# An fp32 attention and two-layer MLP kernel: the sign of half the weight conversions is made by GpSimd instead of VectorE

## The chip, the cores and the metric

The kernel runs on one core of a Trainium2 chip. The metric is the device time of one execution in microseconds, as the median of several runs. TensorE (PE in the profile) multiplies matrices, VectorE (DVE) and ScalarE (ACT) work elementwise, GpSimd (POOL) works elementwise on SBUF only, and SyncE (SP) issues all the DMAs. Each engine takes its own instructions strictly in the order of the program and waits at the first one whose inputs are not there.

## The reference

Three stages follow each other. `q`, `k` and `v` have the shape (4, 8, 576, 64); 4 x 576 = 2304 tokens, each 8 x 64 = 512 wide.

```
scores = where(mask, q @ k.T / 8, -1e9)       # heads 0-3: the last 32 keys; heads 4-7: every 32nd key
x  = softmax(scores) @ v                      # 2304 x 512
x  = relu(x @ w_in)**2 @ w_out                # 512 -> 2048 -> 512
h  = x @ w_in2                                # 512 -> 2048
g  = (a0 + a1 h + a2 h^2 + a3 h^3) / (1 + |b0||h| + |b1| h^2 + 1e-6)
out = g @ w_out2                              # 2048 -> 512
```

The weights arrive as 8-byte floats, and the kernel turns them into 4-byte floats on the chip.

## The kernel before

**Precision.** A matrix product of 4-byte accuracy is built from three fast ones. Each operand is split into a high part (rounded to the fast format) and a low part (the rest), and a tile of the product is the sum of high x high, high x low and low x high. So every weight tile needs `wh` and `wl`, every activation tile `xh`, `xl` or `gh`, `gl`.

**Blocks.** The tokens are worked in five blocks (512, 384, 512, 512 and 384 tokens in the first layer). In a block there are 16 units, one for each 128 of the 2048 hidden features. Unit `f` computes `h` (12 matmuls, line 423), squares it on ScalarE, splits it into `gh` and `gl`, and two units later adds its part to four output accumulators `acc` (12 matmuls, line 468). Names in the listings below carry block and unit: `h_0_2` is block 0, unit 2; `wh_2` and `wl_2` are the weights of unit 2. The second layer is the same with lines 423 and 658.

**Conversion of weights.** The first layer's weights are converted once, while block 0 runs: 32 conversions, (unit, part), part 0 being the columns for `h` and part 1 those for `acc`. Their order is the list `wq`: (0,0), (1,0), (2,0), (0,1), (3,0), (1,1), (4,0), ... alternating from there on, until the last ones are all of part 1. `feed_w` issues two in each unit. One conversion is a chain over three engines (`to_f32`, lines 177 to 192, then `split_w`, line 198):

- ScalarE, line 188: `w` = the absolute value of the upper 4-byte word, scaled, which moves the exponent into place;
- VectorE, line 189: `bits` = `w` shifted left by 3, without the sign bit (`bits` lies in PSUM);
- VectorE, line 190: the sign bit of the upper word is put in;
- VectorE, line 191: the top 3 bits of the lower word are put in; the result is written over the raw tile or over `w`;
- GpSimd, lines 200 and 201: `wh` and then `wl`.

**Attention.** It is cut into 13 pieces (`ORDER`). For a piece, TensorE computes scores into two PSUM banks, VectorE subtracts the maximum (line 339), ScalarE takes the exponential (line 340), VectorE sums (lines 341 to 343), GpSimd scales (line 344), TensorE transposes (line 352), ScalarE copies back (line 354), and TensorE multiplies by `v` (line 361). The tiles are called `eas`/`es` (strided heads) or `eal`/`el` (local heads). Three pieces come before block 0 starts (to about 30 us), three more (numbers 3 to 5) run inside it, the others later. Pieces with a number under `MASK_PE` (line 236) get their mask by a matmul of an identity with the mask into the bank (line 295), onto which the scores are added; for the others VectorE adds the mask to the scores (line 329).

**The order of work.** The code is written unit by unit; a scheduler then puts the instructions of each engine in an order by its own estimate of when they can start, apart from those that the kernel pins with `keep_in_program_order` (the attention matmuls of the first three pieces, the conversions' ScalarE step in block 0, the second layer's elementwise work). Changed instructions can so change places with others on their engine. `fill` (line 486) puts matmuls of ones into TensorE's stream in front of some steps of the first pieces.

**The end.** In the second layer `split2` (line 640) makes `gh` on ScalarE and `gl` on GpSimd (line 645) for each unit. The last unit is (4, 14), a double unit of 256 tokens; the last 24 matmuls of the program use it.

Of the kernel before, what the change touches and what calls it, by code (L numbers as in the profile page):

```python
# [9 lines left out]
F32 = mybir.dt.float32  # L10
# [4 lines left out]
ALU = mybir.AluOpType  # L15
# [13 lines left out]
NB2 = len(WIDTHS2)  # L29
FSTEP = [512 // w for w in WIDTHS2]  # L30
STARTS2 = tuple(sum(WIDTHS2[:j]) for j in range(NB2 + 1))
NF = DFF // P
# [89 lines left out]
def moe_kernel(ctx, tc, qs, vs, ql, vl, w1, w2, a, b, masks, eye, out):  # L122
    nc = tc.nc
# [49 lines left out]
    def in_order(which, ins):  # L173
        if which and block0[0]:
            tc.keep_in_program_order(ins)

    def to_f32(layer, f, part, raw, place=None):

        lo, hi = raw[:, :, 0], raw[:, :, 1]
        w = stage.tile([P, DM], I32, tag="w32", bufs=3, name=f"w32_{layer}_{f}_{part}")
        bits, to = w, w
        if layer == 0 and place:
            to = hi
        if layer == 0:
            bits = psum_w.tile([P, DM], I32, tag="bits", name=f"bits{f}_{part}")
        in_order(layer == 0, nc.scalar.activation(w.bitcast(F32), hi.bitcast(F32), AF.Abs, scale=2.0**-112))
        nc.vector.tensor_scalar(bits, w, 3, 0x7FFFFFFF, ALU.logical_shift_left, ALU.bitwise_and)
        nc.vector.scalar_tensor_tensor(bits, hi, -0x80000000, bits, ALU.bitwise_and, ALU.bitwise_or)  # L190
        nc.vector.scalar_tensor_tensor(to, lo, 29, bits, ALU.logical_shift_right, ALU.bitwise_or)
        return to.bitcast(F32)

    def w_place(layer, f):
        wt[layer, f] = tuple(wpool.tile([P, 2 * DM], F32R, tag=f"w{c}{f}", name=f"w{c}{layer}_{f}") for c in "hl")
        return wt[layer, f]

    def split_w(wh, wl, wf):

        nc.gpsimd.tensor_scalar(wh, wf, 1.0, 0.0, ALU.mult, ALU.add)  # L200
        nc.gpsimd.tensor_tensor(wl, wf, wh.bitcast(F32), ALU.subtract)
# [31 lines left out]
    ORDER = [("s", 0, 2), ("s", 0, 3), ("l", 0), ("l", 1), ("s", 1, 2), ("s", 1, 3), ("l", 2),  # L233
             ("s", 2, 2), ("s", 2, 3), ("l", 3), ("s", 3, 2), ("s", 3, 3), ("l", 4)]
    pieces = [Piece(n, *x) for n, x in enumerate(ORDER)]
    HEAD, MASK_PE = 3, 6
    for p in pieces[:HEAD]:
        p.pinned = True
    pieces[0].homes = ("l8", "l9")
# [262 lines left out]
    def load_co():  # L502
# [9 lines left out]
    homes = [  # L512
        ("h8", 0), ("h9", 0), ("h15", 0), ("h14", 0), ("h13", 0), ("h12", 0), ("l15", 0), ("l14", 0), ("l13", 0), ("l12", 0), ("l9", 1), ("l8", 1),
        ("h11", 1), ("l11", 1), ("h10", 1), ("l10", 1),
    ]
    homes += [(x, 1) for x in ("h12", "h13", "h14", "h15", "l15", "l14", "l13", None, None, None, "h15", "l15")] + [(None, 1)] * 4
    raws = []

    def load_raw(done):

        while len(raws) < min(len(wq), done + AHEAD):
            k = len(raws)
            place, free = homes[k]
            if phase < free or place and any(homes[i][0] == place for i in range(done, k)):
                break
            raws.append(load_w(0, *wq[k], place=place and "w" + place))

    fed = [0]
    AHEAD = 8

    def feed_w(n):
        for _ in range(n):
            load_raw(fed[0])
            if fed[0] < len(wq):
                f, part = wq[fed[0]]
                c = slice(part * DM, (part + 1) * DM)
                wh, wl = wt[0, f] if part else w_place(0, f)
                split_w(wh[:, c], wl[:, c], to_f32(0, f, part, raws[fed[0]], homes[fed[0]][0]))
                fed[0] += 1

    phase, under_way[0] = 0, 2_200_000
# [14 lines left out]
    load_qk(pieces[3])  # L556
    at_out(P0)
    feed_w(1)
    at_transpose(P1, 0)
    at_transpose(P1, 1)  # L560
    at_values(P1)
    at_out(P1)
    load_v(pieces[3])
    feed_w(1)
    at_transpose(P2, 0)
    at_transpose(P2, 1)
    at_values(P2)
    at_out(P2)
    phase, under_way[0] = 1, 0
    load_raw(fed[0])  # L570
    feed_w(1)
    steps = [(j, f) for j in range(NB) for f in range(NF)]
    prev = []
# [3 lines left out]
    def spill_w(f, part):  # L577

        wf = to_f32(1, f, part, load_w(1, f, part))
        parts = [stage.tile([P, DM], F32R, tag="w32", bufs=3, name=f"sp{c}{f}_{part}") for c in "hl"]  # L580
        split_w(*parts, wf)
        for z, t in enumerate(parts):
            nc.sync.dma_start(w2_dram[z, f][:, part * DM : (part + 1) * DM], t.bitcast(F32))
# [5 lines left out]
    keep = tc.keep_in_program_order  # L589
# [50 lines left out]
    def split2(n):  # L640
        if len(open2) > n:
            j, f, rq = open2.pop(0)
            gh, gl = (l2.tile([P, 512], F32R, tag=f"g{c}2", name=f"g{c}1_{j}_{f}", bufs=4) for c in "hl")
            keep(nc.scalar.copy(gh, rq))  # L644
            keep(nc.gpsimd.tensor_tensor(gl, rq, gh.bitcast(F32), ALU.subtract))  # L645
            gt[1, j, f] = gh, gl

    def o_unit2(j, f):
# [26 lines left out]
    def unit2(j, f):  # L675
        ps = psum.tile([P, 512], F32, tag="ps", name=f"h1_{j}_{f}")
        for d in range(FSTEP[j]):
            h_unit(1, j, f + d, ps)
        act2(j, f, ps)
        split2(2)  # L680
        if j + 1 < NB2 and f in X_AT[j > 0]:
            load_x1(j + 1, X_AT[j > 0].index(f))
        prev2.append((j, f))
# [71 lines left out]
    for j, f in [(j, f) for j in range(NB2) for f in range(0, NF, FSTEP[j])][EARLY:]:  # L755
        unit2(j, f)
        while len(prev2) > LAG2:
            o_unit2(*prev2.pop(0))
    multiply2()
    split2(1)  # L760
    split2(0)
    for u in prev2:
        o_unit2(*u)
# [19 lines left out]
```

## Time and profile before

| | us |
|---|---|
| median of 3 runs | 856.35 |
| lowest, highest | 855.86, 857.38 |
| the profiled execution | 857.55 |
| its span, first to last instruction | 855.8 |
| block 0 of the first layer | about 30 to 137 |
| second layer alone | about 475 to 852 |

A sum that starts from the trace starts from 857.55 us. The page lists busy time by engine; queries give the stretch, the waits and the single instructions. TensorE is called busy while any matmul is in flight, and the matmuls overlap in its pipeline: a 512-wide matmul is shown as 0.39 us, but in a dense stretch the next one starts 0.23 us later. So starts are compared, not lengths. VectorE's instructions overlap a little too.

### The profile page before, as it was taken

The numbers are of one execution on the slowest core, as the hardware profiler recorded it, in microseconds if no ns is written. First come the engines' busy times: TensorE is split into PE (matmuls) and PEld (weight loads), VectorE is DVE, ScalarE is ACT, GpSimd is POOL, SyncE is SP. The second block draws the span as 40 slices with busy tenths as digits, with TensorE's granted clock in tenths as the row PEclk, the third lists the DMA queues.
The fourth block names the chain that finished last, engine by engine and source line by source line (L and its number), as shares of the span: only waits on it lengthen the run. The fifth ranks groups of instructions, "written<-read, shape, count | busy, mean of one in ns | idle before, by whom it ended". The sixth has DMA issues, their size and how long they took to land.

```text
span 855.8 us, 14872 instructions
## 1 busy us (share of the span) xinstructions
PE 846.5 (99%) x5762; PEld 720.0 (84%) x5762; DVE 600.3 (70%) x688; ACT 453.6 (53%) x821; POOL 523.2 (61%) x468
## 2 busy tenths in 40 slices
PE   7999999999999999999999999999999999999998
PEld 4788889999888888889999888888888888888896
DVE  5899856556556555552127688888888888888885
ACT  3556534333333343333346566676667666766673
POOL 1687754455444465664334687778777777777664
PEclk9999999999999999999999999999999999999999
DMA  9972535555343374565774300010001000100010
GB/s 338 358 246 78 171 122 200 165 178 188 109 148 106 101 242 156 193 197 194 263 256 148 137 24 25 12 62 13 14 12 62 7 7 6 57 1 0 1 51 25
DMA packets 38246, 99.99 MB, mean 117 GB/s; under 512 B 4384, under 2 KB 8224, under 8 KB 38176
## 3 DMA queue, kind: packets, MB, share of 16 engines
q1 hardware_dynamic: 38176, 99.05, 34.3%
q8 instruction: 45, 0.74, 0.3%
q14 instruction: 25, 0.20, 0.1%
HBM read 72.82 MB, written 26.21 MB: 116 GB/s over the span
## 4 chain that ended last, share of the span: by engine, by line
PE 98%; DVE 1%; DMA 0%; ACT 0%; issue 0%; POOL 0%; SPq 0%; ACTq 0%; POOLq 0%
PE h L423 46%; PE acc L468 23%; PE acc L658 23%; PE ps_vl L361 1%; PE ps_sl L300 1%; PE ps_vs L361 1%; PE ps_ss L300 1%; PE ps_tl L352 1%; PE ps_ts L352 1%; DMA cst<-in_masks 0%; DVE sm L330 0%; PE ps_tl L490 0%; DVE sm L341 0%; PE ps_ss L295 0%; PE ps_sl L295 0%; DVE eal L339 0%
## 5 line engine op out<-in xcount | busy, mean ns | idle before, releaser
L423 PE MATMUL h<-xh,wh 128*128 128x512 f32 (+2 forms) x640 | 237.0, 371 | 0.0
L423 PE MATMUL h<-xh,wl 128*128 128x512 f32 (+2 forms) x640 | 235.6, 368 | 0.0
L423 PE MATMUL h<-xl,wh 128*128 128x512 f32 (+2 forms) x640 | 235.6, 368 | 0.0
L629 DVE RECIPROCAL h<-w 128x512 f32<-128x512 f32 x67 | 224.6, 3353 | 0.0
L624 POOL TENSOR_TENSOR p<-p,hs 128x512 f32<-128x512 f32 x67 | 86.9, 1297 | 97.6 <-ACT p L622 97.5
L423 PEld LDWEIGHTS h<-xh,wh 128*128 128x128 f32 x640 | 120.4, 188 | 18.3 <-issue 0.5
L423 PEld LDWEIGHTS h<-xh,wl 128*128 128x128 f32 x640 | 120.3, 188 | 17.7
L423 PEld LDWEIGHTS h<-xl,wh 128*128 128x128 f32 x640 | 120.4, 188 | 17.5
L468 PE MATMUL acc<-gh,wh 128*128 128x512 f32 (+1 forms) x320 | 118.2, 369 | 0.0
L468 PE MATMUL acc<-gh,wl 128*128 128x512 f32 (+1 forms) x320 | 117.7, 368 | 0.0
L468 PE MATMUL acc<-gl,wh 128*128 128x512 f32 (+1 forms) x320 | 117.6, 367 | 0.0
L658 PE MATMUL acc<-wh,gh 128*128 128x512 f32 x288 | 112.2, 389 | 0.0
L658 PE MATMUL acc<-wh,gl 128*128 128x512 f32 x288 | 112.2, 389 | 0.0
L658 PE MATMUL acc<-wl,gh 128*128 128x512 f32 x288 | 112.1, 389 | 0.0
L619 ACT ACTIVATE sq<-h 128x512 f32<-128x512 f32 x72 | 43.0, 597 | 128.3 <-PE h L423 122.0
L446 POOL TENSOR_TENSOR gl<-r,gh 128x512 fp32r<-128x512 f32 (+1 forms) x59 | 69.5, 1178 | 63.6 <-ACT gh L445 58.4
L627 DVE SCALAR_TENSOR_TENSOR p<-p,co,h 128x512 f32<-128x512 f32 x72 | 53.6, 745 | 69.2 <-POOL p L624 69.2
L438 ACT ACTIVATE r<-h 128x512 f32<-128x512 f32 (+1 forms) x75 | 41.8, 558 | 112.7 <-PE h L423 112.7
L442 DVE TENSOR_TENSOR r<-r 128x512 f32<-128x512 f32 (+1 forms) x59 | 43.6, 739 | 76.3 <-ACT r L438 76.2
L645 POOL TENSOR_TENSOR gl<-rq,gh 128x512 fp32r<-128x512 f32 x72 | 93.4, 1298 | 3.2 <-ACT gh L644 3.2
L626 POOL TENSOR_TENSOR w<-w,sq 128x512 f32<-128x512 f32 x66 | 85.5, 1296 | 0.0
L445 ACT CAST gh<-r 128x512 fp32r<-128x512 f32 (+1 forms) x75 | 43.7, 583 | 57.4 <-DVE r L442 56.9
(115 smaller groups left out, 1324.2 us busy)
## 6 DMA issues: line engine op xcount, KB each, us to landing
wraw<-in_w SPq DMA_DIRECT2D x64, 512.0 KB, 4.3
w_scratch<-sph SPq DMA_DIRECT2D x32, 256.0 KB, 3.9
w_scratch<-spl SPq DMA_DIRECT2D x32, 256.0 KB, 3.2
wh<-w_scratch SPq DMA_DIRECT2D x16, 512.0 KB, 3.9
wl<-w_scratch SPq DMA_DIRECT2D x16, 512.0 KB, 5.3
qks<-in_qs SPq DMA_DIRECT2D x8, 585.0 KB, 5.2
out_dram<-osb SPq DMA_DIRECT2D x18, 256.0 KB, 2.4
xraw<-x_scratch SPq DMA_DIRECT2D x16, 256.0 KB, 2.7
```

The lines of the kernel that those rows point to most:

```text
L423: nc.tensor.matmul(ps[:, :n], w[:, c], x, start=(kk == 0 and i == 0), stop=(kk == KT - 1 and i == 2))
L442: nc.vector.tensor_tensor(h, h, h, ALU.mult)
L445: last_act = nc.scalar.copy(gh, h).ins
L446: low = lambda: (nc.vector if psum_h or j == 0 else nc.gpsimd).tensor_tensor(gl, h, gh.bitcast(F32), ALU.subtract)
L468: nc.tensor.matmul(acc[j][e][:, : WIDTHS[j]], w[:, c], g, start=(f == 0 and i == 0), stop=(f == NF - 1 and i == 2))
L619: keep(nc.scalar.activation(sq, h, AF.Square))
L624: keep(nc.gpsimd.tensor_tensor(p1, p1, hs, ALU.mult))
L626: keep((nc.vector if last else nc.gpsimd).tensor_tensor(w, w, sq, ALU.add))
L627: keep(nc.vector.scalar_tensor_tensor(p1, p1, a1, h, ALU.add, ALU.mult))
L629: keep(nc.vector.reciprocal(h, w))
L645: keep(nc.gpsimd.tensor_tensor(gl, rq, gh.bitcast(F32), ALU.subtract))
L658: nc.tensor.matmul(p, g[:, cg], w[:, c], start=(f + d + i == 0), stop=(f + d == NF - 1 and i == 2))
```

## The change

There are three edits.

First, conversions with an even place in `wq` (16 of the 32) get `zero=True`. GpSimd multiplies the upper word, read as a 4-byte float, by 2^-126 twice, in place: what is left is a zero with the sign of the weight (line 191 of the changed file). VectorE then makes `bits` in one step, `w` shifted left by 3, or'ed with that zero (line 192), and puts in the lower word as before. The conversion thus has one ScalarE, one new GpSimd, two VectorE and the two old GpSimd steps.

Second, `MASK_PE` goes from 6 to 4: pieces 4 and 5, both strided, get their mask from VectorE.

Third, the very last `gl`, that of unit (4, 14), is made by VectorE.

```diff
+        if zero:
+            z = hi.bitcast(F32)
+            nc.gpsimd.tensor_scalar(z, z, 2.0**-126, 2.0**-126, ALU.mult, ALU.mult)
+            nc.vector.scalar_tensor_tensor(bits, w, 3, hi, ALU.logical_shift_left, ALU.bitwise_or)
+        else:
+            nc.vector.tensor_scalar(bits, w, 3, 0x7FFFFFFF, ALU.logical_shift_left, ALU.bitwise_and)
+            nc.vector.scalar_tensor_tensor(bits, hi, -0x80000000, bits, ALU.bitwise_and, ALU.bitwise_or)
         nc.vector.scalar_tensor_tensor(to, lo, 29, bits, ALU.logical_shift_right, ALU.bitwise_or)
...
-    HEAD, MASK_PE = 3, 6
+    HEAD, MASK_PE = 3, 4
...
-                split_w(wh[:, c], wl[:, c], to_f32(0, f, part, raws[fed[0]], homes[fed[0]][0]))
+                split_w(wh[:, c], wl[:, c], to_f32(0, f, part, raws[fed[0]], homes[fed[0]][0], fed[0] % 2 == 0))
...
-            keep(nc.gpsimd.tensor_tensor(gl, rq, gh.bitcast(F32), ALU.subtract))
+            keep((nc.vector if (j, f) == (NB2 - 1, NF - FSTEP[-1]) else nc.gpsimd).tensor_tensor(gl, rq, gh.bitcast(F32), ALU.subtract))
```

The file grows by five lines, so line 200 of before is 205, 201 is 206, 295 is 300, 344 is 349, 423 is 428 and so on.

GpSimd's order at the start of block 0. In the names, `wraw_3_0` is the raw tile of conversion (3,0), the numbers at the end are buffers. Before:

```order
L344 TENSOR_TENSOR eas_3_1_228<-eas_3_1_228,sm_82 128x6x54
L344 TENSOR_TENSOR eal_0_314<-eal_0_314,sm_79 128x512
L344 TENSOR_TENSOR eal_1_346<-eal_1_346,sm_80 128x512
L200 TENSOR_SCALAR wh_0_369<-wraw_0_0_108 128x512
L201 TENSOR_TENSOR wl_0_370<-wraw_0_0_108,wh_0_369 128x512
L200 TENSOR_SCALAR wh_1_433<-wraw_1_0_110 128x512
L201 TENSOR_TENSOR wl_1_434<-wraw_1_0_110,wh_1_433 128x512
L200 TENSOR_SCALAR wh_2_535<-wraw_2_0_112 128x512
```

With the change:

```order
L349 TENSOR_TENSOR eas_3_1_228<-eas_3_1_228,sm_82 128x6x54
L191 TENSOR_SCALAR wraw_0_0_108<-wraw_0_0_108 128x512
L349 TENSOR_TENSOR eal_0_314<-eal_0_314,sm_79 128x512
L349 TENSOR_TENSOR eal_1_346<-eal_1_346,sm_80 128x512
L191 TENSOR_SCALAR wraw_2_0_112<-wraw_2_0_112 128x512
L205 TENSOR_SCALAR wh_0_369<-wraw_0_0_108 128x512
L206 TENSOR_TENSOR wl_0_370<-wraw_0_0_108,wh_0_369 128x512
L191 TENSOR_SCALAR wraw_3_0_116<-wraw_3_0_116 128x512
L205 TENSOR_SCALAR wh_1_433<-wraw_1_0_110 128x512
L206 TENSOR_TENSOR wl_1_434<-wraw_1_0_110,wh_1_433 128x512
L205 TENSOR_SCALAR wh_2_535<-wraw_2_0_112 128x512
```

The new steps (line 191) stand between the old ones; that of conversion (3,0), which is the fifth of `wq`, stands ahead of the `wh` of (1,0), which is the second.

TensorE's order where block 0 begins (`ps_sl` are the score banks of piece 3). Before:

```order
L423 MATMUL h_0_0_567<-xh_0_527,wh_0_369 128x512
L423 MATMUL h_0_1_612<-xh_0_527,wh_1_433 128x512
L295 LDWEIGHTS cst
L295 MATMUL ps_sl_0_631<-cst 128x384
L295 LDWEIGHTS cst
L295 MATMUL ps_sl_1_632<-cst 128x384
L423 MATMUL h_0_0_567<-xl_0_528,wh_0_369 128x512
L423 MATMUL h_0_0_567<-xh_0_527,wl_0_370 128x512
```

With the change:

```order
L428 MATMUL h_0_0_567<-xh_0_527,wh_0_369 128x512
L428 MATMUL h_0_1_612<-xh_0_527,wh_1_433 128x512
L300 LDWEIGHTS cst
L300 MATMUL ps_sl_0_631<-cst 128x384
L300 LDWEIGHTS cst
L300 MATMUL ps_sl_1_632<-cst 128x384
L428 MATMUL h_0_2_724<-xh_0_527,wh_2_535 128x512
L428 MATMUL h_0_0_567<-xl_0_528,wh_0_369 128x512
```

The first matmul of unit 2 has moved up, ahead of eleven matmuls of unit 0 and eleven of unit 1; apart from this and the mask matmuls, TensorE's order is the same.

TensorE's order at the scores of piece 4. Before:

```order
L468 MATMUL acc_0_3_746<-gh_0_3_798,wl_3_558 128x512
L295 LDWEIGHTS cst
L295 MATMUL ps_ss_2_0_989<-cst 128x324
L295 LDWEIGHTS cst
L295 MATMUL ps_ss_2_1_990<-cst 128x324
L300 MATMUL ps_ss_2_0_989<-qks_2_699 64x54
```

With the change:

```order
L473 MATMUL acc_0_3_746<-gh_0_3_798,wl_3_558 128x512
L305 MATMUL ps_ss_2_0_989<-qks_2_699 64x54
L305 MATMUL ps_ss_2_1_990<-qks_2_699 64x54
L305 MATMUL ps_ss_2_0_989<-qks_2_699 64x54
L305 MATMUL ps_ss_2_1_990<-qks_2_699 64x54
```

Two loads and two matmuls have gone; piece 5 reads the same.

## Rows read from the trace of the kernel before

**Rows 1.** Page, part 1: busy us, share of the span, instructions.

```profile
PE 846.5 (99%) x5762; PEld 720.0 (84%) x5762; DVE 600.3 (70%) x688; ACT 453.6 (53%) x821; POOL 523.2 (61%) x468
```

**Rows 2.** What TensorE waited for: us in total, times, longest.

```profile
PE ps_ts L352 <- POOL eas L344: 1.9, 2, 1.4
...
PE ps_ss L295 <- DMA cst<-in_masks: 0.2, 1, 0.2
```

**Rows 3.** Busy us by stretch: length, engines, granted TensorE clock, DMA share, GB/s.

```profile
19.74:23.15 3.41, 1.93 (x47) 1.38 (x48) 3.16 (x12) 2.79 (x9) 1.41 (x2) 1.00 1.02 386
23.15:26.57 3.42, 3.42 (x13) 2.11 (x11) 2.90 (x8) 1.67 (x6) 2.37 (x3) 0.50 0.98 318
26.57:29.98 3.41, 2.91 (x132) 2.35 (x131) 2.05 (x3) 1.67 (x4) 2.19 (x3) 1.00 0.93 327
29.98:33.39 3.41, 3.41 (x17) 2.48 (x16) 3.22 (x5) 0.57 (x2) 1.24 (x2) 1.00 0.99 379
...
40.00:60.00 20.00, 20.00 (x181) 16.58 (x180) 19.52 (x37) 13.62 (x25) 17.16 (x18) 1.00 0.74 262
```

**Rows 4.** Timeline of ScalarE, 26 to 28 us: start, length, what, [idle before].

```profile
26.76 0.58 ACT L354 COPY eal<-ps_tl 128x512 f32<-128x512 f32 x1 [1.12 <-PE ps_tl L352]
27.24 0.69 ACT L188 ACTIVATE w<-wraw 128x512 f32<-128x512 f32 x1
```

**Rows 5.** Timeline of GpSimd, 24.6 to 27 us.

```profile
24.75 0.65 POOL L200 TENSOR_SCALAR wh<-wraw 128x512 fp32r<-128x512 f32 x1 [0.97 <-DVE wraw L191]
25.48 1.29 POOL L201 TENSOR_TENSOR wl<-wraw,wh 128x512 fp32r<-128x512 f32 x1
```

**Rows 6.** Timeline of VectorE, 27 to 29 us.

```profile
27.99 0.69 DVE L190 SCALAR_TENSOR_TENSOR bits<-wraw,bits 128x512 int32<-128x512 int32 x1
```

**Rows 7.** Timeline of TensorE, 30 to 31.4 us.

```profile
30.21 0.70 PE L423 MATMUL h<-xh,wh 128*128 128x512 f32 x2
30.75 0.50 PE L295 MATMUL ps_sl<-cst 128*128 128x384 bf16 x2
30.95 0.53 PE L423 MATMUL h<-xl,wh 128*128 128x512 f32 x1
```

**Rows 8.** Timelines of TensorE at masked scores (61 us) and unmasked ones (127 us).

```profile
61.64 0.45 PE L295 MATMUL ps_ss<-cst 128*128 128x324 bf16 x2
62.02 0.92 PE L300 MATMUL ps_ss<-qks 64*64 64x54 f32 x48
...
126.94 0.39 PE L468 MATMUL acc<-gh,wl 128*128 128x512 f32 x1
127.26 1.48 PE L300 MATMUL ps_sl<-qkl 64*32 64x64 f32 x128
```

**Rows 9.** Timelines of TensorE, then GpSimd, end of the block's last matmuls.

```profile
848.95 0.39 PE L658 MATMUL acc<-wh,gh 128*128 128x512 f32 x1
849.18 0.39 PE L658 MATMUL acc<-wl,gh 128*128 128x512 f32 x1
...
849.85 0.40 PE L658 MATMUL acc<-wh,gh 128*128 128x512 f32 x1
...
848.17 1.29 POOL L645 TENSOR_TENSOR gl<-rq,gh 128x512 fp32r<-128x512 f32 x1 [3.24 <-ACT gh L644]
```

**Rows 10.** One line's instructions: ns min/median/max, first and last start, forms.

```profile
L446 DVE TENSOR_TENSOR gl<-r,gh x16: 678/688/1271, 35.8 to 121.7; 128x512 fp32r<-128x512 f32 x16
...
L189 DVE TENSOR_SCALAR bits<-w x32: 680/694/695, 19.2 to 116.5; 128x512 int32<-128x512 int32 x32
...
L329 DVE TENSOR_TENSOR ps_ss<-ps_ss,cst x8: 493/494/495, 153.1 to 260.5; 128x324 f32<-128x324 f32 x8
```

**Rows 11.** Timelines of GpSimd (44 to 50 us), TensorE, and line 352's instructions.

```profile
45.65 2.14 POOL L344 TENSOR_TENSOR el<-el,sm 128x384 f32<-128x384 f32 x2
...
48.56 1.73 POOL L201 TENSOR_TENSOR wl<-wraw,wh 128x512 fp32r<-128x512 f32 x1
...
48.32 0.82 PE L352 MATMUL ps_tl<-ident,el 128*128 128x128 f32 x6
...
70.35 0.73 POOL L344 TENSOR_TENSOR es<-es,sm 128x324 f32<-128x324 f32 x1 [1.05 <-ACT gh L445]
...
L352 PE MATMUL ps_ts<-ident,es x36: 271/273/273, 73.9 to 272.4; 128*128 128x128 f32 x36
```

More of the change, by code (lines that the diff above doesn't have):

```diff
@@ L175, in in_order, with to_f32 @@
             tc.keep_in_program_order(ins)
-    def to_f32(layer, f, part, raw, place=None):
+    def to_f32(layer, f, part, raw, place=None, zero=False):
         lo, hi = raw[:, :, 0], raw[:, :, 1]
@@ L188, in to_f32 @@
         in_order(layer == 0, nc.scalar.activation(w.bitcast(F32), hi.bitcast(F32), AF.Abs, scale=2.0**-112))
-        nc.vector.tensor_scalar(bits, w, 3, 0x7FFFFFFF, ALU.logical_shift_left, ALU.bitwise_and)
-        nc.vector.scalar_tensor_tensor(bits, hi, -0x80000000, bits, ALU.bitwise_and, ALU.bitwise_or)
+        if zero:
[5 more added lines that the diff above has]
+            nc.vector.scalar_tensor_tensor(bits, hi, -0x80000000, bits, ALU.bitwise_and, ALU.bitwise_or)
         nc.vector.scalar_tensor_tensor(to, lo, 29, bits, ALU.logical_shift_right, ALU.bitwise_or)
```

## The prediction

> **What bounds the kernel now.** I read the busy shares first, then the waits, then the stretches, and only then single instructions. TensorE is busy 846.5 of 855.8 us [rows 1]. Its list of waits has six entries, the longest of 1.9 us, the last of 0.2 [rows 2]; all of them lie ahead of 28 us, in the first three attention pieces. From 30 us on TensorE starts one matmul behind the other. VectorE is nearly full in block 0 as well, 19.52 of 20 us between 40 and 60, and GpSimd 17.16 [rows 3], but no TensorE wait names them there: their work is early enough. So a change can gain only by taking matmuls away from TensorE, by closing a hole in the first 30 us or at the end, and it loses whatever new hole it makes. Removing VectorE time alone is worth nothing in this trace.
>
> A measurement of this kernel can tell about 0.2% from no change, 1.7 us.
>
> **The mask matmuls.** In piece 4 the two mask matmuls begin at 61.64 and the scores at 62.02, 0.38 us. Where scores follow a 512-wide matmul without masks, they begin 0.32 us after its start [rows 8], of which 0.23 is the spacing of such matmuls from 848.95 to 849.18 [rows 9], so 0.09 is the price of the switch. Each piece gives 0.38 - 0.09 = 0.29, both 0.58 us, on the path. The masks go to VectorE: four additions of 0.49 [rows 10], 1.98 us. What hides them: 16 conversions lose a step of 0.69 [rows 10], 11 us of VectorE time over block 0, and the piece's own slack. GpSimd finishes the second half of piece 4 at 70.35 + 0.73 = 71.08, and the transposes that use it start at 73.9 [rows 11], 2.8 us later; two masks (1.0 us), and one new GpSimd step that now stands between the halves (0.7), fit. Without that cover the piece would be late by up to 1 us; I take nothing.
>
> **The last `gl`.** TensorE's matmuls at 849.18 and the next but one at 849.85 are 0.67 apart where two spacings of 0.23 make 0.46 [rows 9]: it waited 0.21 us for GpSimd's `gl`, 848.17 to 849.46. The same subtraction on VectorE takes 0.69 [rows 10] and would end at 848.86, before TensorE asks for it at 849.41. VectorE has nothing else there but the copy of the first finished bank, which comes later. Gain 0.21 us, on the path.
>
> **The conversions, at the start of block 0.** VectorE's saving is off the path, so the question is what the new GpSimd steps hold up. GpSimd's order now has the new step of conversion (3,0) ahead of `wh_1`. It needs ScalarE's absolute value of (3,0), and that one stands behind a copy which itself waits for a transpose: it runs from 27.24 to 27.93 [rows 4]. Nothing in the change makes it earlier, since TensorE and ScalarE have the same order up to there. GpSimd is then free: `wh_0` and `wl_0`, which began at 24.75, end by 26.77 [rows 5], and their VectorE steps are fewer than before. So GpSimd waits until 27.93 + 0.08 (its gap between two instructions, 24.75 + 0.65 to 25.48 [rows 5]) and then works without a break:
>
> - the new step, 28.01 to 28.66, at 0.65 us;
> - `wh_1`, 28.74 to 29.39, still ahead of its first use after 30.21 [rows 7];
> - `wl_1`, 29.47 to 30.76;
> - `wh_2`, 30.84 to 31.49.
>
> VectorE's result for (2,0) is ready by then: its two remaining steps take the places that ended at 27.99 + 0.69 = 28.68 [rows 6] at the latest, since the change's order puts both directly behind conversion (1,0).
>
> TensorE now wants `wh_2` at once: the first matmul of `h_0_2` stands in front of the one that started at 30.95 [rows 7]. It cannot start before 31.55, so TensorE stands still for some 0.5 us (0.45 to 0.6, since the second mask matmul ahead of it is not quite done at 30.95). That matmul itself is only moved and costs nothing. This is a new hole on the path: +0.5 us.
>
> The new step is not in the trace. The nearest row is the one-input step on GpSimd with the same tile and the same stride of its input, 0.65 [rows 5]; it differs by a strided output and by a multiplication in place of an addition. The other end is the two-input step, 1.29 [rows 5]. Below 0.65 there is no row that would let 512 elements pass faster. I take 0.65; at 1.29 the hole is 0.5 + 0.64 = 1.14 us.
>
> **The rest of block 0.** GpSimd gets 16 steps of 0.65 + 0.08, 11.7 us, over some 90 us. Between 40 and 60 us, where it was busiest, 17.16 [rows 3] becomes 17.16 + 3 x 0.73 = 19.4 of 20: nearly full, but TensorE's supply has slack, since two conversions with one new step take GpSimd 2 x (0.65 + 1.29 + 0.16) + 0.73 = 4.9 us and a unit's 24 matmuls take TensorE 24 x 0.23 = 5.5. The tightest place is piece 3: GpSimd ended its scaling at 45.65 + 2.14 = 47.79 and TensorE took the first transposes at 48.32 [rows 11], the second half about 0.3 later. Two new steps now stand between the two halves there. If they add their 2 x 0.73 to 47.79 in full, the second half ends at 49.25, and TensorE, 0.5 late, wants it at about 49.1 (48.32 + 0.3 + 0.5); VectorE's shorter queue ahead of the scaling gives a part of the 1.46 back. I take 0, and 0.6 as the other end.
>
> A collision speaks against the change here. VectorE's subtraction of `gl` in block 0, both inputs in SBUF, takes 0.69 as a rule and up to 1.27 [rows 10], and GpSimd's `wl` at 48.56, beside one of them, took 1.73 instead of 1.29 [rows 11]: about 0.4 to 0.6 us is lost on one side when they meet. The fused VectorE step has both inputs in SBUF too (the step that it replaces had one in PSUM), so 16 new meetings can cost some 7 us, shared by the two engines. The Trainium skill, page "SBUF — State Buffer", section "Who interferes with whom", says why: a VectorE instruction with two SBUF inputs and a GpSimd instruction that reads SBUF exclude each other on a shared port, and the later one waits whole. By that rule each of the 16 fused steps meets GpSimd whenever it is busy, and if GpSimd were always the later one, a conversion's new work there would cost it up to 0.73 + 0.6 = 1.3 us; that leaves the sum as it is and is what gives the second rival below its chance. The trace agrees as far as the one pair shows. At 30 us no fused step runs beside the four GpSimd steps counted above, so the hole there is the same with or without it.
>
> **The sum.** -0.58 - 0.21 + 0.5 = -0.29 us, from 857.55 (span 855.8 and 1.75 around it) to 857.26. The profiled execution lay 1.2 us above the median of the runs, which the change doesn't touch: 856.35 - 0.29 = 856.1.
>
> **The rivals.**
>
> *No hole at 31 us* (chance 0.17). TensorE comes to block 0 a little later, or the new step is done sooner, and only the two gains are left: -0.79, 855.6. For it: waits ahead of 28 us vary with when DMAs land, at a DMA share near 1.0 [rows 3]. Against it: ScalarE's step moves along with TensorE.
>
> *GpSimd falls behind* (0.13). The collisions and the new steps make the second half of piece 3 late by 0.6, and another 0.5 is lost at one more place: -0.29 + 1.1 = +0.8, 857.2. For it: 19.4 of 20 us. Against it: 4.9 against 5.5 us a unit.
>
> *Slower: the hole grows and the clock falls* (0.10). After a stretch in which TensorE was busy for 1.93 of 3.41 us, the granted clock was 0.50 for the next 3.42, its lower level of 1.2 GHz; after one with 2.91 of 3.41 it stayed at 1.00 [rows 3]. If the new step costs 1.29, the hole of 1.14 comes close behind the idle time around 27 us. A stretch at half clock loses half of its 3.42 us, 1.7. In sum -0.79 + 1.14 + 1.7 = +2.05, 858.4. [...] Against it: the one-input row says 0.65.
>
> *Faster: a half-clock stretch goes* (0.11). The idle time ahead of 23.15 belongs to waits of the second and third piece. Were it shorter by chance of the new order, that stretch would run at full clock: -0.29 - 1.7 = -2.0, 854.4. For it: VectorE's queue at 19 to 27 us loses two steps. Against it: TensorE's waits there name ScalarE and the like, whose order does not change.
>
> **How the numbers follow.** The forecast has a chance of 0.49. The range leaves out most of the two last rivals, 0.2: 854.9 to 857.9. The likeliest case has its own range of 855.5 to 856.8, from a hole of 0.45 to 1.14 and the spread of the median. Faster by over 0.2% (under 854.6) is the last rival, 0.11, and a little of the first with a lucky median, 0.01; slower (over 858.1) is the third, 0.10, and 0.01 of the second. The same: 0.77.
>
> **What would show it.** Right: a gap of about 0.5 us in front of the fifth matmul of block 0's start, released by GpSimd's `wh_2`, with GpSimd's new step for (3,0) starting at about 28.0; scores of pieces 4 and 5 directly behind `acc` matmuls; even spacing of 0.23 at the end; new steps of 0.65. Wrong: TensorE waits beyond 32 us that name GpSimd or VectorE, a new step of 1 us or more, a granted clock below 1.00 after 30 us, or 23.15 to 26.57 at another clock.

## The result, and the profile after

The changed kernel takes 863.47 us (median of 11 runs, 860.36 to 868.49), the kernel before 856.35 (11 runs beside it, 855.08 to 860.92): the ratio is 1.0078, 95% interval 1.0055 to 1.0101. It is slower by 7.1 us; the forecast was 856.1, its range ended at 857.9, and slower had a chance of 0.11.

Single runs differ by the granted clock, which lay between 0.990 and 1.000 over a whole run, so sizes under 2 us are compared below among runs at 0.999 or more ("at full clock"): 854.85 for the kernel before (42 of the 91 runs beside the experiments), 860.51 for the changed one (4 of 11), 5.7 us apart; such runs of the kernel before spread from 854.13 to 855.97, so differences of medians below some 0.5 us mean little.

Page of the kernel after: busy us by engine, and the share of each engine in the chain that ended last.

```profile
PE 845.2 (98%) x5753; PEld 718.7 (84%) x5758; DVE 606.4 (71%) x677; ACT 453.2 (53%) x821; POOL 539.1 (63%) x483
...
PE 88%; DVE 5%; POOL 3%; ACT 1%; issue 1%; DMA 0%; DVEq 0%; POOLq 0%
```

Against [rows 1], VectorE has 11 instructions fewer and yet 6.1 us more of busy time (four of its instructions, 1.9 us, are the masks); GpSimd has 15 instructions and 15.9 us more. TensorE's 98% in place of 99% is the loss: the span is 859.9. These are TensorE's waits in the kernel after that [rows 2] did not have (us in total, times, longest):

```profile
PE h L428 <- POOL wl L206: 1.2, 1, 1.2
PE h L428 <- DVE es L344: 1.1, 1, 1.1
...
PE ps_ss L305 <- issue: 0.7, 1, 0.7
PE h L428 <- ACT r L443: 0.7, 1, 0.7
PE h L428 <- POOL wh L205: 0.7, 1, 0.7
...
PE ps_tl L357 <- POOL el L349: 0.3, 1, 0.3
```

In [rows 2] no wait lay behind 28 us; here six do, and each names an engine that I had called early enough, or goes back to one (as is seen below). Where they lie is seen in the stretches of the kernel after (length, busy of TensorE, weight loads, VectorE, ScalarE, GpSimd, clock, DMA share, GB/s):

```profile
40.00:60.00 20.00, 19.66 (x179) 16.00 (x178) 19.15 (x31) 13.20 (x25) 17.85 (x19) 1.00 0.74 264
60.00:80.00 20.00, 18.87 (x130) 15.22 (x129) 18.11 (x31) 10.82 (x21) 16.83 (x19) 1.00 0.42 137
80.00:100.00 20.00, 18.03 (x161) 14.17 (x160) 19.26 (x33) 7.80 (x17) 16.10 (x19) 1.00 0.33 108
100.00:120.00 20.00, 19.28 (x128) 15.61 (x127) 17.08 (x25) 10.80 (x22) 17.43 (x17) 1.00 0.45 143
```

TensorE is 20.00 busy between 40 and 60 us in [rows 3]; now it lacks 0.34, 1.13, 1.97 and 0.72 us in four stretches in which the clock is at 1.00. From 120 us on it is full again. Measured as start spacing beyond the usual, block 0 has holes of 0.83 us at 30, 0.5 at 48, 1.3 at 68, 0.9 and 0.3 at 88, 1.3 at 95 and 0.9 at 109, together 6.0. Less the 0.8 that masks and tail give back, that is 5.2, near the 5.7 at full clock.

**The hole at 30 us** stands where the prediction put it, but GpSimd's part differs. GpSimd, a VectorE step beside it, then TensorE, kernel after:

```profile
25.19 1.32 POOL L206 TENSOR_TENSOR wl<-wraw,wh 128x512 fp32r<-128x512 f32 x1
26.59 1.14 POOL L191 TENSOR_SCALAR wraw<-wraw 128x512 f32<-128x512 f32 x1
27.81 0.66 POOL L205 TENSOR_SCALAR wh<-wraw 128x512 fp32r<-128x512 f32 x1
28.56 1.30 POOL L206 TENSOR_TENSOR wl<-wraw,wh 128x512 fp32r<-128x512 f32 x1
29.83 0.65 POOL L205 TENSOR_SCALAR wh<-wraw 128x512 fp32r<-128x512 f32 x1
...
26.50 0.70 DVE L192 SCALAR_TENSOR_TENSOR bits<-w,wraw 128x512 int32<-128x512 int32 x1
...
29.35 0.50 PE L300 MATMUL ps_sl<-cst 128*128 128x384 bf16 x2
30.53 0.50 PE L428 MATMUL h<-xh,wh 128*128 128x512 f32 x1 [0.68 <-POOL wh L205]
```

The order is the forecast one: new step, `wh_1`, `wl_1`, `wh_2`, then the matmul. It starts about 1.4 us earlier than I had it, TensorE too: GpSimd does not stand until ScalarE has the absolute value, which was done at 25.68 instead of 27.93, but goes on 0.08 us behind `wl_0`. And the new step takes 1.14 instead of 0.65: a fused step started 0.09 us ahead of it. Of the 16 new steps two took over 1 us, those at 26.59 and at 75.06 (1.01), and both began while a fused step ran; the other 14 took 0.64 to 0.70. The hole is 0.83 where 0.5 was forecast and 1.14 the other end.

**The hole at 68 us** is the pattern of those that were not forecast. GpSimd and then VectorE, kernel after:

```profile
63.58 0.65 POOL L191 TENSOR_SCALAR wraw<-wraw 128x512 f32<-128x512 f32 x1
64.31 1.18 POOL L205 TENSOR_SCALAR wh<-wraw 128x512 fp32r<-128x512 f32 x1
...
64.26 0.70 DVE L192 SCALAR_TENSOR_TENSOR bits<-w,wraw 128x512 int32<-128x512 int32 x1 [1.30 <-POOL wraw L191]
64.99 0.69 DVE L196 SCALAR_TENSOR_TENSOR wraw<-wraw,bits 128x512 int32<-128x512 int32 x1
65.60 1.83 DVE L451 TENSOR_TENSOR gl<-r,gh 128x512 fp32r<-128x512 f32 x1
67.36 0.89 DVE L334 TENSOR_TENSOR ps_ss<-ps_ss,cst 128x324 f32<-128x324 f32 x2
68.16 0.88 DVE L335 TENSOR_REDUCE sm<-ps_ss 128x6 f32<-128x324 f32 x2
68.97 0.48 DVE L344 TENSOR_TENSOR es<-ps_ss,sm 128x324 f32<-128x324 f32 x1
```

VectorE stood for 1.30 us until GpSimd had done the new step of this conversion; then its `gl`, beside a GpSimd that works without a break, took 1.83 us instead of 0.69. The piece's masks, maxima and subtractions, two each, come behind that. The first subtraction is the last line; the second runs from 69.37 to 69.85. A subtraction is the last VectorE step that reads its half's scores in their PSUM bank, and TensorE's next unit takes over the bank of the first half. TensorE, kernel after:

```profile
68.07 0.39 PE L473 MATMUL acc<-gh,wl 128*128 128x512 f32 x1
69.59 0.47 PE L428 MATMUL h<-xh,wh 128*128 128x512 f32 x1 [1.13 <-DVE es L344]
```

It starts 0.15 us behind the end of the first subtraction, 69.44, while the second still runs. The kernel before, same place, VectorE's two subtractions and TensorE's same unit:

```profile
65.95 0.49 DVE L339 TENSOR_TENSOR es<-ps_ss,sm 128x324 f32<-128x324 f32 x1
...
66.94 0.50 DVE L339 TENSOR_TENSOR es<-ps_ss,sm 128x324 f32<-128x324 f32 x1
...
68.23 0.39 PE L468 MATMUL acc<-gh,wl 128*128 128x512 f32 x1
68.46 0.39 PE L423 MATMUL h<-xh,wh 128*128 128x512 f32 x1
```

There the first half's bank was free at 66.44 and wanted at 68.46: 2.0 us of slack, which no list of waits shows because nothing waited. (The 1.0 us in the expectation of `e2_mask` below goes by the second subtraction.) At piece 5 it is the same: in the kernel before the first subtraction ended at 91.08 and the unit began at 93.35. In the one after, VectorE's first subtraction and TensorE's unit, which could have started at 95.42:

```profile
96.12 0.48 DVE L344 TENSOR_TENSOR es<-ps_ss,sm 128x324 f32<-128x324 f32 x1
...
96.74 0.47 PE L428 MATMUL h<-xh,wh 128*128 128x512 f32 x1 [1.17 <-POOL wl L206]
```

The unit again starts 0.15 us behind the end of the first subtraction, 96.60. The view names GpSimd's `wl`, one that ended at 96.70. But counted along `wq` that is the `wl` of unit 12, and the one that this unit, 11, reads had ended at 89.95.

**The holes at 88 us**, in front of piece 5's scores, carry no name in the view. The scores start at 88.63, 0.1 us behind a subtraction `xl` of VectorE that ended at 88.53 and stood behind a `gl` of 1.83 us; in experiment 1 the view names `xl` at this place.

**The hole at 109 us** goes through ScalarE. Kernel after, VectorE, ScalarE and TensorE:

```profile
107.59 1.16 DVE L192 SCALAR_TENSOR_TENSOR bits<-w,wraw 128x512 int32<-128x512 int32 x1
...
108.78 0.71 ACT L188 ACTIVATE w<-wraw 128x512 f32<-128x512 f32 x1 [1.59 <-DVE bits L192]
109.38 0.59 ACT L443 ACTIVATE r<-h 128x512 f32<-128x512 f32 x1
...
110.12 0.47 PE L428 MATMUL h<-xh,wh 128*128 128x512 f32 x1 [0.72 <-ACT r L443]
```

ScalarE waits until the fused step gives back the tile of an absolute value, and the `r` that empties a PSUM bank for TensorE stands behind it in ScalarE's order.

**Masks and tail** did what was forecast. Piece 4 in the kernel after:

```profile
61.56 0.39 PE L473 MATMUL acc<-gh,wl 128*128 128x512 f32 x1
61.88 0.80 PE L305 MATMUL ps_ss<-qks 64*64 64x54 f32 x40
```

The scores begin 0.32 us behind the last matmul, the forecast spacing without masks. In the last `acc` matmuls the starts are 0.23 apart throughout; the 0.67 of [rows 9] is gone.

### The profile page after: what moved, and what is told of

It reads as the page before. It is cut to its first block, busy times and chain, and to the rows that moved or that the text cites. A ratio compares the mean times of both kernels' runs of the same rounds, so it can differ in the third digit from the quotient of the medians.

```text
span 859.9 us, 14848 instructions
## 1 busy us (share of the span) xinstructions
PE 845.2 (98%) x5753; PEld 718.7 (84%) x5758; DVE 606.4 (71%) x677; ACT 453.2 (53%) x821; POOL 539.1 (63%) x483
## 4 chain that ended last, share of the span: by engine, by line
PE 88%; DVE 5%; POOL 3%; ACT 1%; issue 1%; DMA 0%; DVEq 0%; POOLq 0%
PE h L428 42%; PE acc L663 23%; PE acc L473 20%; POOL wl L206 1%; DVE gl L451 1%; DVE bits L192 1%; POOL wh L205 1%; DVE wraw L196 1%; PE ps_sl L305 1%; PE ps_vl L366 1%; DVE sm L335 1%; POOL wraw L191 1%; DVE bits L195 0%; PE ps_ss L305 0%; PE ps_ss L495 0%
```

## The experiments

The theory at the start was that the conversions alone cost the time; the rivals were the masks that now sit on VectorE, the meetings of the fused step with GpSimd, and GpSimd's added busy time.

**1. The three edits apart.** The conversions alone:

```
-    HEAD, MASK_PE = 3, 4
+    HEAD, MASK_PE = 3, 6
-            keep((nc.vector if (j, f) == (NB2 - 1, NF - FSTEP[-1]) else nc.gpsimd).tensor_tensor(gl, ...))
+            keep(nc.gpsimd.tensor_tensor(gl, ...))
```

> Only the conversions changed (new GpSimd step, fused VectorE step); masks of pieces 4 and 5 by matmul and the last gl on GpSimd, as before. Theory A (the conversions' new steps and their meetings with GpSimd on the shared port make VectorE late): about +4 us over before, holes in TensorE's stream at 30, 48, and about 1 us each near 68, 88 and 110, gl on VectorE at 1.6 to 1.8 us. Theory B (the masks keep score banks of PSUM for longer): about +1 us, only the holes at 30 and 48.

Measured: 863.24 against 856.02, ratio 1.0084 (1.0052 to 1.0116); 860.04 in the one run at full clock. TensorE's new waits:

```profile
PE h L428 <- ACT r L443: 2.7, 1, 2.7
...
PE h L428 <- POOL wh L205: 1.0, 1, 1.0
PE ps_ss L300 <- DVE xl L390: 0.8, 1, 0.8
```

The conversions make the whole loss. The holes lie elsewhere than in the kernel after, but are of the same kinds: a PSUM bank that ScalarE or VectorE empties late, and `wh_2` at 30 us. VectorE waits 5.1 us for the new step, in three places; 2.6 of it are at 120 us, behind the last hole.

The masks alone (`MASK_PE = 3, 4` in the kernel before):

> Only MASK_PE 4: pieces 4 and 5 masked by VectorE, all else as before. Theory A: VectorE is late by two masks only, 0.8 us, and the slack of the score banks before (1.0 us: the last subtraction ended at 67.44, unit 7 began at 68.46) covers it: -0.5 us, no new hole. Theory B: holes of 1 us each at 68 and 95, about +1.5 us net.

Measured: 855.26, ratio 1.0002 (0.9977 to 1.0027); at full clock 854.28, 0.57 below the kernel before, as against 0.58 in the sum. No wait over 0.2 us behind 30 us. That the two agree to 0.01 is luck, at a spread of 0.5; the whole-run ratio shows no gain.

The last `gl` alone on VectorE:

> Only the last gl on VectorE. Both theories: -0.2 us, and in the trace even spacing of 0.23 us at the place of the gap at 849.2.

Measured: 854.56, ratio 0.998 (0.9953 to 1.0006); at full clock 854.36, so -0.5 where the sum has -0.21, which is no difference at that spread. Neither of these two edits costs anything, as the sum had it; the third is off.

**2. The fused step without the GpSimd step.** In the changed kernel the new GpSimd instruction is left out, so that the fused step combines the raw upper word (the sign and the weights of 16 conversions are then not the reference's):

```
-            nc.gpsimd.tensor_scalar(z, z, 2.0**-126, 2.0**-126, ALU.mult, ALU.mult)
```

> The changed kernel without the new GpSimd step (the 16 conversions or the raw upper word in, so their weights are wrong): VectorE still saves a step and its fused step still has two SBUF inputs. Theory A in the form 'GpSimd's extra work and the wait for it': all holes in block 0 go, -0.8 us against before. Theory A in the form 'port meetings of the fused step': about half of the holes stay, +2 us. Theory B: the holes at 68 and 95 stay at 1 us each, +1 us.

Measured: 856.23 against 856.02, ratio 1.0002 (0.9982 to 1.0022); at full clock 854.81. Busy us between 20 and 130 us, first the kernel before, then this one:

```profile
20.00:130.00 110.00, 108.28 (x1108) 87.70 (x1109) 93.32 (x171) 59.73 (x116) 75.18 (x77) 0.98 0.57 195
```

```profile
20.00:130.00 110.00, 108.44 (x1088) 88.22 (x1082) 95.85 (x157) 58.92 (x115) 81.48 (x77) 1.00 0.58 204
```

The meetings are real: VectorE has 14 instructions fewer, with four masks of 1.9 us in all among those that it has, and 2.5 us more; GpSimd has the same 77 and 6.3 us more. TensorE has two holes, waits of 0.3 us each. The time is the kernel before's only because this kernel keeps the gain of masks and tail: against experiment 8, which has these two edits alone (854.28), it is +0.5 us. That is at the edge of what these medians can tell, and about a tenth of the loss: the theory that the meetings alone do it falls.

**3. GpSimd's work without its result.** The same 16 GpSimd steps, written to a tile that nothing reads, and the fused step on the raw word (so the weights of 16 conversions are again not the reference's); masks and tail as before the change:

```
+            s = stage.tile([P, DM], BF16, tag="zs", bufs=1, ...)
-            nc.gpsimd.tensor_scalar(z, z, 2.0**-126, 2.0**-126, ALU.mult, ALU.mult)
+            nc.gpsimd.tensor_scalar(s, z, 2.0**-126, 2.0**-126, ALU.mult, ALU.mult)
```

> e1 with the new GpSimd step's result put into a tile that nothing reads (and VectorE's fused step on the raw upper word, so the weights of the 16 conversions are wrong): GpSimd has its 16 extra steps, but no step of VectorE waits for one. If GpSimd's time and its meetings with VectorE on the port are the cause, the time stays near e1's, +5 us over before at an equal clock. If VectorE's wait for GpSimd's queue (5.1 us in e1's trace, over three places) is the cause, it falls to before's time, within 1 us.

Measured: 855.76 against 855.46, ratio 1.0008 (0.9975 to 1.004); at full clock 855.39, +0.5. The same stretch of this kernel:

```profile
20.00:130.00 110.00, 107.84 (x1101) 87.55 (x1094) 92.15 (x151) 58.73 (x114) 90.68 (x92) 1.00 0.58 204
```

GpSimd is as full as in experiment 1 (90.30), the fused steps and the new steps are there, and one hole of 0.97 us is left. What this kernel lacks against experiment 1 is what hangs on the new step's place in the conversion: VectorE waits for it, and it waits for ScalarE, which must have read the word before it is overwritten (GpSimd idles 9.3 us for that in experiment 1, not at all here). With these gone the 16 `gl` are stretched less, too, 17.2 us in all instead of 20.5. All this together is worth 860.04 - 855.39 = 4.7 us; the run does not divide it.

**4. The wait with the old VectorE steps.** GpSimd multiplies the word by 1.0 in place, and VectorE keeps its three steps:

```
+            nc.gpsimd.tensor_scalar(z, z, 1.0, 1.0, ALU.mult, ALU.mult)
```

> The new GpSimd step (a multiplication of the upper word by 1, in place) beside VectorE's three old steps: GpSimd's extra work and VectorE's wait for it stay, VectorE saves nothing and its steps have one SBUF input. If the fused step's two SBUF inputs are needed for the loss, it is within 2 us of before. If GpSimd's queue alone does it, it is as slow as e1 or slower, +6 to +10 us, since VectorE has 16 steps more than in e1.

Measured: 860.94, ratio 1.0044 (1.0006 to 1.0081); at full clock 856.26, +1.4, one hole of 0.99. Only 3 of the 10 runs were at full clock, hence the higher median. Here the GpSimd result is asked for one VectorE step later, and VectorE waited for it 1.0 us in all, against 5.1 in experiment 1. But the fused step with its two SBUF inputs is gone as well, and the median `gl` takes 0.89 us instead of 1.26. So a GpSimd step in the middle of the chain need not cost 5 us; whether the later reader or the missing fused step saves them, this run cannot tell.

**5. The fused step with one SBUF input.** ScalarE puts the absolute value into the PSUM bank that the bits take:

```
+        if zero:
+            w = bits
```

> e1 with ScalarE's w put into the PSUM bank of bits for the 16 conversions, so that VectorE's fused step has one SBUF input. If the port meetings of the fused step are the cause: its mean falls from about 1.0 to 0.7 us and half or more of the 6 us goes. If GpSimd's queue is the cause: less than 1.5 us goes. A risk is the single bank: ScalarE can then write w only after the conversion before it is finished.

Measured: 872.26, ratio 1.0191 (1.0144 to 1.0239). The fused step itself, then what VectorE waited for:

```profile
L194 DVE SCALAR_TENSOR_TENSOR bits<-bits,wraw x16: 692/700/700, 20.9 to 133.8; 128x512 int32<-128x512 int32 x16
```

```profile
DVE bits L194 <- POOL wraw L193: 31.4, 15, 3.3
```

All 16 steps take 0.70 us, as one would expect if the long ones come from the two SBUF inputs. But the single PSUM bank puts the conversions in a row, VectorE waits 31.4 us for GpSimd, and GpSimd is less full (busy 77.0 us between 20 and 130, against 90.3 in experiment 1). On the price of the meetings this says nothing; it shows that the wait, made longer, costs more.

**6. The sign made by ScalarE.** A copy with scale 0 in place of the GpSimd step (the weights of 16 conversions are then not the reference's; what the copy leaves of the sign was not looked into):

```
-            nc.gpsimd.tensor_scalar(z, z, 2.0**-126, 2.0**-126, ALU.mult, ALU.mult)
+            in_order(layer == 0, nc.scalar.activation(z, z, AF.Copy, scale=0.0))
```

> e1 with the signed zero made by ScalarE (a copy with scale 0, in place) instead of GpSimd: VectorE's fused step and its two SBUF inputs stay, GpSimd has no extra work. If GpSimd's extra work is the cause, the time is that of before, within 1 us at an equal clock; if the fused step is, +4 us or more. ScalarE gets 16 x 0.66 us, where it was busy 13.6 of 20 us between 40 and 60.

Measured: 857.51, ratio 1.0017 (0.9994 to 1.004); no run at full clock, no wait of TensorE in block 0, and no hole over 0.3 us (two, at 47 us). With the round trip through GpSimd gone, the large holes are gone too. GpSimd's extra work is gone with it; that the work alone is not the cause is what experiment 3 says.

**7. Fewer conversions the new way.** One in four (8 conversions; masks and tail as before the change), and all but the first three of the 16:

```
+ ..., fed[0] % 4 == 2))
```
```
+ ..., fed[0] % 2 == 0 and fed[0] > 5))
```

> e1 with the new way for every fourth conversion (8 of 32) instead of every second; masks and last gl as before. If VectorE's lost time decides (in e1: 11 us saved, but 5 us on the fused steps, 7 us on gl and 5 us of waiting for GpSimd lost again): half of the sums, about +3 us on VectorE, which its slack in block 0 takes, so within 1.5 us of before. If single new steps placed badly in GpSimd's order decide, the loss goes with their number: about +2.7 us.

> e1 without the new way for the first six conversions, so the step of (3,0) no longer stands ahead of the wh of (1,0); 13 conversions keep it. The hole of 1.0 us at 30 goes; the others stay if they have the same cause as before: 1 us faster than e1, +4 to +5 us over before. If the hole at 30 makes all that follows late, +1 us or less.

Measured: 8 conversions 855.97, ratio 0.9997 (0.997 to 1.0023), at full clock 855.72 (+0.9); 13 conversions 860.59, ratio 1.0067 (1.0036 to 1.0098), at full clock 859.65 (+4.8). With 13 the hole at 30 us is gone, and holes of 0.74, 0.72 and 1.64 at 67, 86 and 108 us stay. So the early hole and the later loss are separate, and the later one is no echo of the early one. From 8 to 13 conversions the loss grows by more than their number. That fits a slack behind which each conversion costs, but the 8 and the 13 also stand at different places, so it is not shown.

**8. The other two edits together, without the conversions** (`MASK_PE = 3, 4` and the last `gl`):

> Both other edits without the conversions: masks of pieces 4 and 5 and the last gl on VectorE. -0.58 and -0.21 add up: -0.8 us against before, no hole in block 0 over 0.3 us. This is the version that should beat both kernels.

Measured: 854.8, ratio 0.9994 (0.9969 to 1.0019); at full clock 854.28, 0.6 below the kernel before and 6.2 below the one after. It is the version to keep, though its gain is too small for a whole-run comparison to show, and the tail's part of it for any comparison here (the masks alone gave 0.57).

**9. `gl` with one SBUF input.** Experiment 1 with `gl` of block 0 read straight from its PSUM bank:

```
-    psum_h = j == NB - 1 and f >= NF - EARLY
+    psum_h = j == 0 or j == NB - 1 and f >= NF - EARLY
```

> e1 with relu and square of block 0 left in the unit's own PSUM bank, so that VectorE's 16 gl steps there have one input in SBUF and one in PSUM. If their meetings with GpSimd on the port carry much of the loss: gl falls from 1.28 to about 0.7 us in the mean, VectorE gets some 7 to 9 us back, and 2 us or more of e1's +5.3 go. If the wait for GpSimd's queue is what decides, less than 1 us goes. A risk: a unit's bank is held until its gl is made, some 2 us longer, and TensorE may wait for banks.

Measured: 859.93, ratio 1.004 (1.0008 to 1.0072); at full clock 859.57. The `gl` line of this kernel, then TensorE's new waits:

```profile
L451 DVE TENSOR_TENSOR gl<-h,gh x21: 537/683/693, 34.8 to 471.4; 128x512 fp32r<-128x512 f32 x16, 128x384 fp32r<-128x384 f32 x5
```

```profile
PE h L428 <- DVE gl L451: 2.1, 2, 1.4
PE h L428 <- POOL wh L205: 1.2, 1, 1.2
```

No `gl` is long any more, but each keeps a PSUM bank until it is done, and TensorE waits 2.1 us for those. VectorE still waits 3.8 us for the new step. Experiment 1's one run at full clock is 0.5 us more, which settles nothing.

## Why the prediction was wrong

**What held.** The masks (scores directly behind `acc`, about -0.6), the even spacing at the end, and the hole at 30 us with its releaser. Its size, 0.83, comes from the new step, which was priced by its one-input neighbour, 0.65, and took 1.14 there. The prediction ruled out a meeting at this place ("no fused step runs beside the four GpSimd steps"), and there was one. Of the signs named for "wrong", three are there: TensorE waits beyond 32 us that name VectorE and GpSimd, a new step over 1 us, and 23.15 to 26.57 at another clock. Over all 16 the new step was 0.65 as a rule; the rows of the kernel after (ns minimum, median, maximum; first and last start):

```profile
L191 POOL TENSOR_SCALAR wraw<-wraw x16: 642/666/1142, 18.5 to 120.6; 128x512 f32<-128x512 f32 x16
...
L192 DVE SCALAR_TENSOR_TENSOR bits<-w,wraw x16: 699/1116/1411, 21.6 to 121.2; 128x512 int32<-128x512 int32 x16
...
L451 DVE TENSOR_TENSOR gl<-r,gh x16: 683/1506/1842, 35.5 to 126.2; 128x512 fp32r<-128x512 f32 x16
```

**The step that failed** is the one headed "The rest of block 0": "I take 0, and 0.6 as the other end". It measured about 5 us (6.0 of holes less the 0.83 at 30), and only the 0.5 at 48 us, piece 3's transposes, lie at the place that the step had priced. Three things went into it:

- *"VectorE's saving is off the path."* I took 11 us out of VectorE and let its queue run ahead. The rows above say otherwise. The median fused step takes 1.12 us where two steps of 0.69 went away, and the median `gl` goes from 0.69 [rows 10] to 1.51. Between 20 and 132 us, fused steps 16.3 us, `gl` 20.7 instead of 13.2, and 3.9 us of waiting for the new step make 16.3 + 7.5 + 3.9 = 27.7 new us against 16 x 2 x 0.69 = 22.1 that went: VectorE has some 5.6 us more to do and to wait for, not 11 less. Of the wait, 2.6 us stand at 121 us, behind the last hole, so some 3 us of this bear on the holes, and the masks' 1.9 come on top. The prediction had the collision, and even its total ("some 7 us"), and then wrote that it "leaves the sum as it is". It priced the new meetings of the fused step only; that `gl`, already there, would be stretched by a GpSimd that no longer pauses was not in it.
- *The dependency.* The working treated the new step as 0.73 us more in GpSimd's queue. It is also a wait in the middle of VectorE's order, for a result at the end of GpSimd's. Experiments 3 and 1 have the same GpSimd and VectorE steps, and differ in where the new one writes and so in what waits for what: +0.5 against +5.2 us.
- *The slack.* I measured it at one consumer, GpSimd's scaling before the transposes (2.8 us). The nearer limit was the PSUM bank of the scores' first half: 2.0 us at piece 4, 2.3 at piece 5. "No TensorE wait names them" was true and told only that the slack was above zero.

**The rivals.** "GpSimd falls behind" had the right direction and the wrong price, +0.8, as it asked only what reaches TensorE from GpSimd directly; of the seven holes (two of them at 88 us) only those at 30 and 48 us do. "Faster: a half-clock stretch goes" came about in the profile of the kernel after, where 23.15 to 26.57 has a clock of 1.00 instead of the 0.50 of [rows 3], and the loss is there all the same. "The hole grows and the clock falls" did not come about in that profile: from 30 us to the last matmul it has no half-clock stretch. But its mechanism is to be seen in experiment 1, behind the hole of 2.66 us. Two stretches of that kernel:

```profile
108.35:111.80 3.45, 1.02 (x5) 0.87 (x6) 3.18 (x5) 2.25 (x4) 2.51 (x4) 1.00 0.32 118
111.80:115.30 3.50, 3.50 (x10) 2.74 (x9) 3.50 (x8) 1.47 (x6) 3.42 (x3) 0.51 0.00 0
```

A stretch with TensorE busy for 1.02 of 3.45 us, then one at 0.51. In that way a hole can cost twice. Whether this makes up the rest of the 7.1 us, beyond the 5.7 at full clock, was not followed run by run and stays open.

**What stays open.** Shown is that the loss comes with the conversions (experiment 1) and goes when the new step no longer stands in their chain (experiment 3). How the 5 us divide between VectorE's wait, GpSimd's wait for ScalarE and the meetings is open. Without the waits the meetings cost 0.5 (experiments 2 and 3); with them but without the long `gl` the loss was still 4.7 (experiment 9), though with a new wait of its own. VectorE's waits ahead of the last hole are only 1.3 us in the kernel after and 2.4 in experiment 1. That waits and meetings need each other is argued from these, not shown. The scheduler also orders each kernel anew, so holes don't keep their places from one to the next.

## What to carry to other kernels

A step handed to another engine is a round trip through that engine's queue: if the giver needs the result in its very next instruction, price the queue ahead of it, not only the step, and look for other work to put between. Before calling a saving off the path, look at every resource that the engine releases, PSUM banks above all, and write down when each is freed and when it is next wanted; a list of waits is silent about a slack of 2 us, and can name the wrong engine when two events fall together. And a nearly full GpSimd stretches instructions that the change does not touch, so price those too.

## What the runs showed of the hardware

- A VectorE step of 128x512 with both inputs in SBUF took 0.69 us alone and up to 1.84 beside a GpSimd that never paused (`gl` above). With one input in PSUM the same subtraction stayed at 0.69 or less in experiment 9, where the fused steps still reached 1.83 (GpSimd busy 86.5 of 110 us); in the kernel after, the 48 conversion steps with one input in SBUF and one in PSUM took 0.70 at most.
- The one-input step on GpSimd, 0.65 us, took 1.14 and 1.01 in the two places where it began while a fused step ran: either side can be the one that is held up.
- In experiment 2 the meetings ate what 16 saved VectorE steps should have freed (2.5 us more busy time, 1.9 of it masks) and made GpSimd 6.3 us busier, and the end moved by 0.5: busy time that grows is not lost one for one.
